# Which products add into their sums by DMA, where x is split, and the order of the last slot, in a three-layer kernel

## The chip, the cores and the metric

The kernel runs on one core of a Trainium2 chip. The metric is the device time of one execution in microseconds, the median of the runs shown. The profile comes from one further execution, taken by the hardware profiler.

## The reference

Linear attention with a normalized output is followed by two layers without biases. The first squares what is left of a ReLU, the second multiplies by a cosine.

```python
kv = np.einsum('bhsd,bhse->bhde', k, v)          # 8 batches, 8 heads, 576 tokens, 64 wide
out = np.einsum('bhsd,bhde->bhse', q, kv)
rms = np.sqrt(np.mean(out * out, axis=-1, keepdims=True) + 1e-06)
x = (out / rms * g_norm)                          # brought to 4608 tokens x 512
h = x @ w_in;  g = np.maximum(h, 0.0) ** 2;  x = g @ w_out      # w_in 512 x 2048
h = x @ w_in2; g = h * np.cos(h);            out = g @ w_out2
```

All of it is float32. The kernel splits operands into a high and a low part and adds up three products (high with high, high with low, low with high).

## The kernel before

**Stage one** runs over nine tiles of 512 tokens and, in each, over parts of the hidden width of the first layer (`layer_in`, `layer_out`, L379 and L416); together they are its chunks. Half of that layer is done here directly, and its partial results are evicted by ScalarE and VectorE into `ev` (L402, L404) and stored to `p_d` (L405). Between the chunks stand the units of attention, whose results `xo` are stored to `x_d`; the conversion of weights, which brings them from their given form into high and low parts and combinations of blocks (L111 to L197); and, for the later token tiles, the loads of x from `x_d` (`load_x`, L227) and the split of x (`split_x`): ScalarE casts the high part (L232), and GpSimd subtracts it from x to give the low part (L233).

**The slots** follow, from about 502 us on: thirty, ten for the rest of the first layer (m=0) and twenty for the second (m=1), each a tile of tokens and one group of the hidden width. The tiles are 512, 512, 512, 384 and 384 wide in one half (there are two halves of each, j). A slot does its matrix products by a scheme with seven products for eight blocks, in the order 0, 1, 3, 2, 5, 4, 6. First products (L508) go into the two banks FA and FB in turn. `keep` (L527), `add` (L533, L537) and `whole` (L545) make four blocks h from them, and ReLU and square (L549, L553) or five steps of the cosine (L557 to L575) make y. They are finished in the order (0,0), (1,1), (0,1), (1,0). `s_block` makes the operand of a second product from the y, with up to two subtractions on VectorE (L591), then splits it: gh is cast by ScalarE (L607), gl subtracted by VectorE (L608). Second products (L631) go into the banks SA and SB in turn, which `drain_product` empties. The operands t1 and t2 of products 2 and 3 are made together, when product 3's operand is due.

`drain_product` has four ways. The first product of many slots is copied by ScalarE into the other bank, as what product 1 then adds to (L650). In the first group of a tile the sums are begun by a copy on ScalarE (L654). Products named in BY_DMA are copied by ScalarE into one of two buffers `part` (L659), and GpSimd issues a DMA that adds them to the sum (L660). All others are added by VectorE (L662). Products 0 and 1 belong to the sum (0,0), 2 and 5 to (1,1), 3 and 4 to (0,1), 6 to (1,0). Only slots with m=1 use the DMA, and the last slot doesn't.

Seven pairs of late weights of the second layer are loaded (L145, SyncE) and converted during the first slots.

**The order.** Every action is given a position on an axis of chunks and slots (`at`, `pos`; PH is a seventh of a slot). Positions are priorities: the order of each engine is set when the program is built, by a scheduler that follows them and its own view of what is ready. SyncE issues nearly all DMAs, in order, so one that waits holds those behind it. Tiles take their memory from pools in the order in which the pools are opened; a tile that takes the memory of another waits until that one has been read.

Of the kernel before, what the change touches and what calls it, by code (L numbers as in the profile page):

```python
# [8 lines left out]
F32 = mybir.dt.float32  # L9
# [4 lines left out]
ALU = mybir.AluOpType  # L14
# [8 lines left out]
def kernel(  # L23
# [205 lines left out]
    def split_x(t, c):  # L229
        h, l = new_x(t, c)  # L230
        src = xraw[t, c // 2][:, c % 2, :]
        nc.scalar.copy(out=h, in_=src)  # L232
        nc.gpsimd.tensor_tensor(out=l, in0=src, in1=as32(h[:]), op=ALU.subtract)  # L233

# [191 lines left out]
    BLOCKS = {(0, 0): 2, (1, 1): 5, (0, 1): 6, (1, 0): 7}  # L426
    S_ORDER = (0, 1, 3, 2, 5, 4, 6)
    BY_DMA = (4, 5, 1, 6)
    SEEDED = 2
# [6 lines left out]

    HOLD = 9
    xb, wi, ws, kept, hs, ys, sums, quads = {}, {}, {}, {}, {}, {}, {}, {}

# [139 lines left out]
    def load_sum(k, d, j):  # L579
# [3 lines left out]
        for b, s0, done, size in pieces(t0 + j * ht, ht, TOK):  # L583
            nc.sync.dma_start(out=e[:, :, done:done + size], in_=p_d[b][:, 2 * d:2 * d + 2, s0:s0 + size])

    def s_block(k, i):
        m, t, q = slots[k]
        b11, b12, b21, b22 = (ys.get((k, b)) for b in ((0, 0), (0, 1), (1, 0), (1, 1)))

        def minus(out, x, y):  # L590
            nc.vector.tensor_tensor(out=out, in0=x, in1=y, op=ALU.subtract)  # L591
            return out

        if i == 3:
            ys[k, "t1"] = minus(t_tile(k, F32, "t"), b12, b11)
            ys[k, "t2"] = minus(t_tile(k, F32, "t"), b22, ys[k, "t1"])
        src = {
            0: lambda: b11,
            1: lambda: b21,
            2: lambda: ys[k, "t1"],  # L600
            3: lambda: ys[k, "t2"],
            4: lambda: b22,
            5: lambda: minus(b12, b22, b12),
            6: lambda: minus(b21, b21, ys[k, "t2"]),
        }[i]()
        gs[k, i] = h, l = [t_tile(k, F32R, f"g{n}") for n in "hl"]
        nc.scalar.copy(out=h, in_=src)  # L607
        nc.vector.tensor_tensor(out=l, in0=src, in1=as32(h), op=ALU.subtract)  # L608
# [77 lines left out]
    class Stream:  # L686
# [10 lines left out]
        def place(self, positions, after, skip=()):  # L697
            for k, (n, item) in enumerate(zip(positions, self.items)):
                steps = (0, 0.07, 0.15, 0.22, 0.3, 0.4, 0.62)
                if n < nA0:  # L700
# [30 lines left out]
    at(pos(0.15), late_stream.advance)  # L731
    late_stream.place([pos(0.45 + 1.05 * k) for k in range(5)] + [pos(9.9), pos(10.85)], 0)

# [15 lines left out]
    for t in range(NDIRECT, NTILE):  # L749
        n0 = t * NH  # L750
        for q in range(2):
            at(n0 - (4 if t == NDIRECT else 5.2) + q, load_x, t, q)
        for c in range(NKC):
# [6 lines left out]
    for k, (m, t, q) in enumerate(slots):  # L760
        if q == 0:
            for a in range(2):
                at(pos(k + (a - 6.8) * PH) if k else nA0 - 9, load_quads, m, t, a)
            for f, i in enumerate(ORDER):
                at(pos(k + X_AT[f] * PH) if k or f > 3 else nA0 - 7 + 1.5 * f, x_block, k, i)
        for f, i in enumerate(ORDER):
            at(pos(k + (f - 2.7) * PH) if k or f > 2 else nA0 - 5 + f / 2, load_wi, k, i)
        for f, i in enumerate(S_ORDER):
            at(pos(k + LAG2 + (f - 2.7) * PH), load_ws, k, i)
            at(pos(k + LAG2 + (f - (1.1 if f == 1 else 1.6)) * PH), s_block, k, i)  # L770
        if not seeded(k):
# [53 lines left out]
    def run_slots():  # L825
# [12 lines left out]
        steps1 = (x for k, i in firsts for x in first_product(k, i))  # L838
        todo = [(k, i) for k in range(len(slots)) for i in S_ORDER]
        steps2 = (x for k, i in todo for x in second_product(k, i))  # L840
# [34 lines left out]
    with ExitStack() as early:  # L875
# [5 lines left out]
        pools["raw"] = right("conv", 2)  # L881
        x_p, g_p, ev_p, pools["t"] = (right(n, b) for n, b in (("x", XB), ("g", 3), ("ev", 2), ("tmp", 8)))
        with tc.tile_pool(name="att", bufs=1, side="right") as att_p:
# [64 lines left out]
```

## Time and profile before

| | us |
|---|---|
| runs, median (lowest, highest) | 1594.09 (1589.73, 1597.51) |
| profiled execution | 1593.9 |
| its span, first to last instruction | 1592.1 |
| TensorE busy | 1542.6 |
| VectorE busy | 1254.8 |
| ScalarE busy | 1107.7 |
| GpSimd busy | 105.5 |

The mean granted clock of TensorE is 0.997 of full speed. To read it: each engine runs its own instructions in order, and semaphores tie them. Idle time of an engine that isn't the bound costs nothing by itself; a wait counts where TensorE has to wait in the end. The rows below give for an instruction its start and length, and in brackets how long its engine stood idle before it and what ended that.

### The profile page before, as it was taken

How to read it: one execution, taken by the hardware profiler on the slowest of the kernel's cores; microseconds unless marked ns; L12 is line 12 of the kernel's file. 1: busy time of each engine (PE TensorE's matmuls, PEld its weight loads, DVE VectorE, ACT ScalarE, POOL GpSimd, SP SyncE). 2: the span in 40 equal slices, each digit the busy share in tenths (PEclk: the TensorE clock that was granted, in tenths of full speed). 3: DMA queues.
4: the chain of work that ended last, by engine and by line, in shares of the span. 5: the costliest groups of instructions: out<-in, count | busy, mean ns of one | idle time of the engine just before them, and what ended most of it. 6: DMA issues, size and time to landing. Idle time of an engine off the chain costs nothing.

```text
span 1592.1 us, 24817 instructions
## 1 busy us (share of the span) xinstructions
PE 1542.6 (97%) x9104; PEld 1349.8 (85%) x9104; DVE 1254.8 (79%) x1676; ACT 1107.7 (70%) x1568; POOL 105.5 (7%) x117
## 2 busy tenths in 40 slices
PE   5999999999999999999999999999999999999997
PEld 4777777778887777888998899999998999999997
DVE  7988788788885898987879868766876687687576
ACT  6977677775444666665656778877887777778774
POOL 1100101111000000000000000000000001011010
PEclk9999999999999999999999999999999999999999
DMA  9758889866678989998999779987998799999994
GB/s 325 269 168 230 261 259 284 238 204 208 195 230 298 309 283 338 319 385 263 336 355 341 279 229 269 280 266 227 268 271 263 227 262 297 333 302 275 323 296 116
DMA packets 229160, 433.13 MB, mean 272 GB/s; under 512 B 18608, under 2 KB 144816, under 8 KB 229040
## 3 DMA queue, kind: packets, MB, share of 16 engines
q1 hardware_dynamic: 218624, 397.21, 74.2%
q0 software_dynamic: 10416, 34.35, 10.7%
q8 instruction: 72, 1.18, 0.3%
q14 instruction: 48, 0.39, 0.1%
HBM read 317.72 MB, written 81.79 MB: 251 GB/s over the span
## 4 chain that ended last, share of the span: by engine, by line
PE 77%; DMA 8%; DVE 6%; issue 4%; ACT 4%; SPq 0%; DVEq 0%; ACTq 0%; POOLq 0%
PE SB L631 14%; PE SA L631 14%; PE FB L508 13%; PE FA L508 13%; PE acc L416 10%; PE l L379 9%; DMA sum<-part 2%; PE o L379 1%; DMA ws_d<-raw 1%; PE ss L379 1%; DVE gl L608 1%; DMA xraw<-x_d 1%; DMA q<-in_qT 1%; DMA p_d<-ev 1%; DMA raw<-in_wA 1%
## 5 line engine op out<-in xcount | busy, mean ns | idle before, releaser
L508 PE MATMUL FA<-xh,wi 128*128 128x512 f32 (+1 forms) x840 | 300.0, 371 | 8.0 <-ACT h L545 3.3
L508 PE MATMUL FB<-xh,wi 128*128 128x512 f32 (+1 forms) x840 | 299.3, 370 | 0.0
L631 PE MATMUL SA<-ws,gh 128*128 128x256 f32 x1008 | 230.3, 282 | 5.5 <-ACT gh L607 5.5
L631 PE MATMUL SB<-ws,gh 128*128 128x256 f32 x1008 | 229.3, 282 | 2.0 <-ACT SB L650 1.9
L631 PEld LDWEIGHTS SA<-ws,gh 128*128 128x128 f32 x1008 | 181.9, 190 | 17.3 <-ACT gh L607 6.2
L631 PEld LDWEIGHTS SB<-ws,gh 128*128 128x128 f32 x1008 | 181.0, 189 | 14.0 <-ACT SB L650 3.3
L508 PEld LDWEIGHTS FA<-xh,wi 128*128 128x128 f32 x840 | 157.3, 188 | 20.5 <-ACT h L545 3.9
L575 DVE SCALAR_TENSOR_TENSOR y<-y,h 128x1024 f32<-128x1024 f32 (+1 forms) x80 | 89.3, 1116 | 108.4 <-ACT y L571 108.1
L508 PEld LDWEIGHTS FB<-xh,wi 128*128 128x128 f32 x840 | 157.3, 188 | 11.1
L631 PE MATMUL SB<-ws,gl 128*128 128x256 f32 x504 | 142.4, 282 | 1.5 <-DVE gl L608 1.5
L631 PE MATMUL SA<-ws,gl 128*128 128x256 f32 x504 | 142.4, 282 | 0.6 <-DVE gl L608 0.6
L608 DVE TENSOR_TENSOR gl<-y,gh 128x1024 fp32r<-128x1024 f32 (+1 forms) x100 | 111.2, 1113 | 34.7 <-ACT gh L607 33.5
L660 POOL DMA_DIRECT2D sum<-part x67 | 57.0, 851 | 1101.9 <-DMA wi<-wi_d 535.2
L557 ACT ACTIVATE y<-h,zerob 128x1024 int32<-128x1024 f32 (+1 forms) x80 | 85.3, 1066 | 40.7 <-DVE h L533 40.6
L416 PE MATMUL acc<-gh,wh 128*128 128x512 f32 x288 | 113.6, 395 | 0.0
L416 PE MATMUL acc<-gl,wh 128*128 128x512 f32 x288 | 112.8, 392 | 0.0
L416 PE MATMUL acc<-gh,wl 128*128 128x512 f32 x288 | 112.6, 391 | 0.0
L508 PE MATMUL FA<-xl,wi 128*128 128x512 f32 (+1 forms) x300 | 111.3, 371 | 0.0
L508 PE MATMUL FB<-xl,wi 128*128 128x512 f32 (+1 forms) x300 | 110.9, 370 | 0.0
L607 ACT CAST gh<-y 128x1024 fp32r<-128x1024 f32 (+1 forms) x100 | 95.0, 962 | 12.6 <-DVE y L575 7.4
L631 PE MATMUL SB<-gh,ws 128*128 128x512 f32 (+1 forms) x280 | 100.0, 370 | 2.9 <-ACT SB L650 1.1
L631 PEld LDWEIGHTS SB<-ws,gl 128*128 128x128 f32 x504 | 95.5, 190 | 7.8 <-DVE gl L608 2.4
(172 smaller groups left out, 3775.4 us busy)
## 6 DMA issues: line engine op xcount, KB each, us to landing
wi<-wi_d SPq DMA_DIRECT2D x210, 512.0 KB, 6.8
ws<-ws_d SPq DMA_DIRECT2D x210, 512.0 KB, 6.0
sum<-part POOLq DMA_DIRECT2D x43, 512.0 KB, 8.1
kvld<-in_kv SPq DMA_DIRECT2D x32, 512.0 KB, 6.7
ws_d<-raw SPq DMA_DIRECT2D x24, 448.0 KB, 4.1
q<-in_qT SPq DMA_DIRECT2D x32, 288.0 KB, 4.0
p_d<-ev SPq DMA_DIRECT2D x18, 512.0 KB, 3.8
sum<-part POOLq DMA_DIRECT2D x24, 384.0 KB, 7.9
```

The source lines that it names most:

```text
L379: nc.tensor.matmul(ps, a[:, 0, cs], m[:], start=(c == 0 and k == 0), stop=(c == NKC - 1 and k == 2))
L416: nc.tensor.matmul(o, a[:, cs], m[:], start=(f == 0 and n == 0), stop=(f == NH - 1 and n == 2), skip_group_check=True)
L508: nc.tensor.matmul(ps[:, pp, :], a, b, start=(n == 0 and (i in (0, 2) or i == 1 and not seeded(k))), stop=(n == 5), skip_group_check=True,)
L557: nc.scalar.activation(out=y.bitcast(I32), in_=hs[k, b], func=AF.Identity, bias=zerob)
L575: nc.vector.scalar_tensor_tensor(out=y, in0=y, scalar=-2.0 * math.pi, in1=hs.pop((k, b)), op0=ALU.add, op1=ALU.mult)
L607: nc.scalar.copy(out=h, in_=src)
L608: nc.vector.tensor_tensor(out=l, in0=src, in1=as32(h), op=ALU.subtract)
L631: nc.tensor.matmul(ps[:, b, :], lhs, rhs, start=(n == 0 and (m == 0 or b % 2 == 0) and (i in (0, 2) or i == 1 and not seeded_s(k))), stop= ...
L660: nc.gpsimd.dma_start(out=e, in_=part, accum_op=ALU.add)
```

## The change

Eight things are changed.

1. `split_x` subtracts the low part on VectorE, 28 instructions.
2. BY_DMA is 1, 2 and 4 in place of 4, 5, 1 and 6. Accumulating DMAs, and the copies to `part` on ScalarE, fall from 67 to 48; VectorE has 19 adds more.
3. The last slot runs its second products in the order 0, 2, 3, 4, 5, 1, 6.
4. t1 and t2 are made by a job of their own, placed ahead of product 2's operand.
5. The late pairs are placed otherwise: the first as before, the others in pairs nearer to each other, and the steps of one conversion closer together.
6. x loads in stage one are placed about a chunk sooner (the first of a tile at 6.2 chunks ahead).
7. The x blocks four to seven of the first slot are placed a seventh of a slot later.
8. The pool of `ev` is opened ahead of those of x, g and the temporaries. With that the late raw buffer shares memory with `ev`.

```diff
-        nc.gpsimd.tensor_tensor(out=l, in0=src, in1=as32(h[:]), op=ALU.subtract)
+        nc.vector.tensor_tensor(out=l, in0=src, in1=as32(h[:]), op=ALU.subtract)
...
-    S_ORDER = (0, 1, 3, 2, 5, 4, 6)
-    BY_DMA = (4, 5, 1, 6)
+    BY_DMA = (1, 2, 4)
...
+    def s_order(k):
+        return ORDER if k < len(slots) - 1 else (0, 2, 3, 4, 5, 1, 6)
...
+    def s_sums(k):
+        ys[k, "t1"] = minus(t_tile(k, F32, "t"), ys[k, (0, 1)], ys[k, (0, 0)])
+        ys[k, "t2"] = minus(t_tile(k, F32, "t"), ys[k, (1, 1)], ys[k, "t1"])
...
-        if i == 3:
-            ys[k, "t1"] = minus(t_tile(k, F32, "t"), b12, b11)
-            ys[k, "t2"] = minus(t_tile(k, F32, "t"), b22, ys[k, "t1"])
...
-                steps = (0, 0.07, 0.15, 0.22, 0.3, 0.4, 0.62)
+                steps = (0, 0.06, 0.12, 0.17, 0.23, 0.3, 0.45)
...
-    late_stream.place([pos(0.45 + 1.05 * k) for k in range(5)] + [pos(9.9), pos(10.85)], 0)
+    late_stream.place([pos(n) for n in (0.4, 2.45, 3.07, 4.45, 5.07, 10.5, 11.1)], 0)
...
-            at(n0 - (4 if t == NDIRECT else 5.2) + q, load_x, t, q)
+            at(n0 - (6.2, 3 if t == 2 else 4.2 if t == 3 else 5.1)[q], load_x, t, q)
...
-                at(pos(k + X_AT[f] * PH) if k or f > 3 else nA0 - 7 + 1.5 * f, x_block, k, i)
+                at(pos(k + (X_AT[f] + (0 if k else 1)) * PH) if k or f > 3 else nA0 - 7 + 1.5 * f, x_block, k, i)
...
-        for f, i in enumerate(S_ORDER):
+        for f, i in enumerate(s_order(k)):
             at(pos(k + LAG2 + (f - 2.7) * PH), load_ws, k, i)
-            at(pos(k + LAG2 + (f - (1.1 if f == 1 else 1.6)) * PH), s_block, k, i)
+            at(pos(k + LAG2 + (f - (1.1 if f == i == 1 else 0.9 if f == 2 and i == 3 else 1.6)) * PH), s_block, k, i)
+            if f == 1:
+                at(pos(k + LAG2 + (0.35 if i == 1 else -0.7) * PH), s_sums, k)
...
-        x_p, g_p, ev_p, pools["t"] = (right(n, b) for n, b in (("x", XB), ("g", 3), ("ev", 2), ("tmp", 8)))
+        ev_p, x_p, g_p, pools["t"] = (right(n, b) for n, b in (("ev", 2), ("x", XB), ("g", 3), ("tmp", 8)))
```

What it does to the order of the engines is shown at three places. In these rows stands the line of the program, which is two or three more in the changed kernel, the operation, output and input, and the semaphores it waits for (DMAHW and DMASW: DMAs issued by SyncE and by GpSimd).

**SyncE at the end of stage one.** `raw<-in_wB` is the load of the next late pair, `p_d<-ev` the stores of the last evictions, `sum<-p_d` and `wi`, `ws` loads for the slots. Before:

```order
L492 DMA ws<-ws_d_0_96 128x1024 [waits DMAHW2_49,PE_49]
L145 DMA raw<-in_wB 128x1024 [waits DMAHW3_49,PE_49,Pool_49]
L145 DMA raw<-in_wB 128x2x512 [waits DMAHW4_49]
L487 DMA wi<-wi_d_1_91 128x1024 [waits DMAHW5_49,PE_49]
L584 DMA sum<-p_d_76 128x1024 [waits DMAHW6_49,PE_49]
L492 DMA ws<-ws_d_0_96 128x1024 [waits DMAHW7_49,PE_49]
L487 DMA wi<-wi_d_1_91 128x1024 [waits DMAHW0_49,PE_49]
L405 DMA p_d_84<-ev 128x1024 [waits DMAHW1_49,DVE_49,Activation_49]
L405 DMA p_d_84<-ev 128x1024 [waits DMAHW2_49,DVE_49,Activation_49]
```

After:

```order
L587 DMA sum<-p_d_76 128x1024 [waits DMAHW4_49,PE_49]
L495 DMA ws<-ws_d_0_96 128x1024 [waits DMAHW5_49,PE_49]
L490 DMA wi<-wi_d_1_91 128x1024 [waits DMAHW6_49,PE_49]
L405 DMA p_d_84<-ev 128x1024 [waits DMAHW7_49,DVE_49,Activation_49]
L405 DMA p_d_84<-ev 128x1024 [waits DMAHW0_49,DVE_49,Activation_49]
L587 DMA sum<-p_d_77 128x1024 [waits DMAHW1_49,PE_49]
L495 DMA ws<-ws_d_0_96 128x1024 [waits DMAHW2_49,PE_49]
L145 DMA raw<-in_wB 128x1024 [waits DMAHW7_49,DMAHW3_49,DMAHW0_49]
L145 DMA raw<-in_wB 128x2x512 [waits DMAHW4_49]
```

The raw load stood ahead of the two stores; now it stands behind them and waits for two more DMAs, those of the two stores (DMAHW7 and DMAHW0).

**ScalarE at the same place.** `ev<-acc` are its evictions, L112, L192 steps of the late conversion, `m` and `u` the kept first products. Before:

```order
L112 ACTIVATE e<-e,expb 128x1024 [waits DVE_49]
L402 COPY ev<-acc_5641 128x512 [waits DMAHW5_49,PE_49]
L402 COPY ev<-acc_5649 128x512 [waits DMAHW6_49,PE_49]
L481 CAST xh<-xraw 128x1024 [waits DMAHW2_49,DMAHW1_49,DMAHW4_49,DVE_49,Activation_49]
L527 ACTIVATE m_5919<-FA 128x1024 [waits PE_49]
L481 CAST xh<-xraw 128x1024 [waits DMAHW7_49,DMAHW0_49]
L549 ACTIVATE h<-h 128x1024 [waits DVE_49]
L553 ACTIVATE h<-h 128x1024 [waits Activation_49]
L527 ACTIVATE u_5959<-FA 128x1024 [waits PE_49]
L481 CAST xh<-xt 128x1024
L192 CAST wh<-raw 128x768 [waits DMAHW4_49,DMAHW3_49]
L527 ACTIVATE m_5995<-FB 128x1024 [waits PE_49]
```

After:

```order
L402 COPY ev<-acc_5641 128x512 [waits DMAHW5_49,PE_49]
L402 COPY ev<-acc_5649 128x512 [waits DMAHW6_49,PE_49]
L530 ACTIVATE m_5914<-FA 128x1024 [waits DVE_49,PE_49,Activation_49]
L484 CAST xh<-xraw 128x1024 [waits DMAHW4_49]
L484 CAST xh<-xraw 128x1024 [waits DMAHW7_49,DMAHW0_49]
L552 ACTIVATE h<-h 128x1024 [waits DVE_49]
L530 ACTIVATE u_5965<-FA 128x1024 [waits PE_49]
L556 ACTIVATE h<-h 128x1024 [waits Activation_49]
L112 ACTIVATE e<-e,expb 128x1024 [waits DMAHW7_49,DMAHW0_49,DVE_49]
L192 CAST wh<-raw 128x768 [waits DMAHW4_49,DMAHW3_49,DVE_49]
L192 CAST wh<-raw 128x1024 [waits DVE_49]
L530 ACTIVATE m_5993<-FB 128x1024 [waits PE_49]
```

The conversion's L112 stood ahead of the evictions and one cast L192 ahead of `m<-FB`; now all three of its steps stand between the second relu step and `m<-FB`, and the first m stands ahead of the two casts of x.

**VectorE in a slot of width 384.** Before, near 1433 us of the profile:

```order
L533 SCALAR_TENSOR_TENSOR h<-FA,u_14334 128x2x384 [waits PE_49]
L608 TENSOR_TENSOR gl<-y,gh 128x2x384 [waits Activation_49]
L482 TENSOR_TENSOR xl<-xt,xh 128x2x384
L561 SCALAR_TENSOR_TENSOR y<-y,h 128x2x384 [waits Activation_49]
L575 SCALAR_TENSOR_TENSOR y<-y,h 128x2x384 [waits Activation_49]
L463 TENSOR_TENSOR xt<-xraw,xt 128x2x384
L575 SCALAR_TENSOR_TENSOR y<-y,h 128x2x384 [waits Activation_49]
L608 TENSOR_TENSOR gl<-y,gh 128x2x384 [waits Activation_49]
```

After, the same place:

```order
L536 SCALAR_TENSOR_TENSOR h<-FA,u_14306 128x2x384 [waits PE_49]
L610 TENSOR_TENSOR gl<-y,gh 128x2x384 [waits Activation_49]
L485 TENSOR_TENSOR xl<-xt,xh 128x2x384
L564 SCALAR_TENSOR_TENSOR y<-y,h 128x2x384 [waits Activation_49]
L578 SCALAR_TENSOR_TENSOR y<-y,h 128x2x384 [waits Activation_49]
L664 TENSOR_TENSOR sum<-SA,sum 128x768 [waits DMASW4_49,PE_49]
L610 TENSOR_TENSOR gl<-y,gh 128x2x384 [waits Activation_49]
L578 SCALAR_TENSOR_TENSOR y<-y,h 128x2x384 [waits Activation_49]
```

Product 5 was copied for the DMA; now its add stands here, behind the cosine step and ahead of gl, and waits for DMASW4, the accumulating DMA of product 2 of the same slot.

## Rows read from the trace of the kernel before

**Rows 1.** The page: busy us, share of the span and count of each engine.

```profile
PE 1542.6 (97%) x9104; PEld 1349.8 (85%) x9104; DVE 1254.8 (79%) x1676; ACT 1107.7 (70%) x1568; POOL 105.5 (7%) x117
```

**Rows 2.** What TensorE waited for: us in total, times, longest us.

```profile
PE SA L631 <- ACT gh L607: 5.5, 3, 3.5
PE ss L316 <- DVE m L329: 4.4, 3, 1.5
PE FA L508 <- ACT h L545: 3.3, 1, 3.3
PE SB L631 <- ACT SB L650: 3.0, 3, 1.5
PE FA L508 <- ACT m L527: 2.8, 2, 1.4
```

**Rows 3.** Timeline, ScalarE: start, us, instruction, [idle before <- what ended it].

```profile
1465.15 0.78 ACT L659 COPY part<-SB 128x768 f32<-128x768 f32 x1
...
1476.50 0.80 ACT L659 COPY part<-SB 128x768 f32<-128x768 f32 x1 [4.88 <-DMA sum<-part]
```

**Rows 4.** Timeline, GpSimd, the same stretch: the issue of an accumulating DMA.

```profile
1466.23 0.85 POOL L660 DMA_DIRECT2D sum<-part  x1 [8.68 <-ACT part L659]
```

**Rows 5.** Stretches: us, busy of five engines, then PEclk, DMA share, GB/s.

```profile
1481.50:1485.50 4.00, 3.96 (x18) 3.96 (x19) 3.90 (x6) 2.45 (x4) 0.00 (x0) 0.61 0.80 205
1571.00:1575.00 4.00, 3.92 (x18) 3.71 (x18) 2.80 (x5) 2.09 (x3) 0.00 (x0) 0.57 0.00 0
```

**Rows 6.** Timeline, SyncE's queue: the last stores of p_d.

```profile
502.70 0.92 SPq L405 DMA_DIRECT2D p_d<-ev  x2
```

**Rows 7.** Timeline, ScalarE: the first cast behind the evictions.

```profile
508.41 1.05 ACT L481 CAST xh<-xraw 128x1024 fp32r<-128x1024 f32 x1 [6.09 <-DMA p_d<-ev]
```

**Rows 8.** Timeline, TensorE: the sixth first product of the first slot begins.

```profile
518.74 0.39 PE L508 MATMUL FB<-xh,wi 128*128 128x512 f32 x1
```

**Rows 9.** Timeline, VectorE: conversion of the first late pair, first and last step.

```profile
499.48 0.69 DVE L111 TENSOR_SCALAR e<-raw 128x1024 uint32<-128x1024 uint32 x1 [3.42 <-PE acc L416]
...
505.66 1.55 DVE L175 TENSOR_TENSOR raw<-raw 128x256 f32<-128x256 f32 x4
```

**Rows 10.** DMA issues: count, KB each, median us from issue to landing.

```profile
sum<-part POOLq DMA_DIRECT2D x43, 512.0 KB, 8.1
...
sum<-part POOLq DMA_DIRECT2D x24, 384.0 KB, 7.9
...
raw<-in_wB SPq DMA_DIRECT2D x14, 512.0 KB, 5.5
```

**Rows 11.** Timeline, TensorE: products 5 and 6 begin, width 512, then 384.

```profile
986.37 0.28 PE L631 MATMUL SA<-ws,gh 128*128 128x256 f32 x1
...
997.57 0.28 PE L631 MATMUL SA<-ws,gh 128*128 128x256 f32 x1
...
1371.32 0.28 PE L631 MATMUL SA<-ws,gh 128*128 128x256 f32 x1
...
1379.76 0.28 PE L631 MATMUL SA<-ws,gh 128*128 128x256 f32 x1
```

**Rows 12.** Timeline, TensorE: waits in the last slot's second products.

```profile
1570.08 0.38 PE L631 MATMUL SA<-ws,gh 128*128 128x256 f32 x1 [3.52 <-ACT gh L607]
1571.07 0.54 PE L631 MATMUL SA<-ws,gl 128*128 128x256 f32 x1 [0.61 <-DVE gl L608]
...
1575.97 0.35 PE L631 MATMUL SA<-ws,gh 128*128 128x256 f32 x1 [0.98 <-ACT gh L607]
```

**Rows 13.** Timeline, VectorE: an add into a sum, width 384.

```profile
1574.91 0.96 DVE L662 TENSOR_TENSOR sum<-SA,sum 128x768 f32<-128x768 f32 x1 [1.17 <-PE SA L631]
```

**Rows 14.** Timeline, VectorE, stage one: conversion steps under a GpSimd subtraction, then gl.

```profile
338.72 1.67 DVE L116 SCALAR_TENSOR_TENSOR w<-raw,w 128x512 uint32<-128x512 uint32 x1
340.31 1.78 DVE L122 SCALAR_TENSOR_TENSOR e<-raw,e 128x512 uint32<-128x512 uint32 x1
342.02 0.68 DVE L394 TENSOR_TENSOR gl<-g,gh 128x512 fp32r<-128x512 f32 x1
```

More of the change, by code (lines that the diff above doesn't have):

```diff
@@ L584, in load_sum, with minus @@
             nc.sync.dma_start(out=e[:, :, done:done + size], in_=p_d[b][:, 2 * d:2 * d + 2, s0:s0 + size])
+    def minus(out, x, y):
+        nc.vector.tensor_tensor(out=out, in0=x, in1=y, op=ALU.subtract)
+        return out
+    def s_sums(k):
+        ys[k, "t1"] = minus(t_tile(k, F32, "t"), ys[k, (0, 1)], ys[k, (0, 0)])
+        ys[k, "t2"] = minus(t_tile(k, F32, "t"), ys[k, (1, 1)], ys[k, "t1"])
     def s_block(k, i):
-        m, t, q = slots[k]
         b11, b12, b21, b22 = (ys.get((k, b)) for b in ((0, 0), (0, 1), (1, 0), (1, 1)))
-        def minus(out, x, y):
-            nc.vector.tensor_tensor(out=out, in0=x, in1=y, op=ALU.subtract)
-            return out
-        if i == 3:
-            ys[k, "t1"] = minus(t_tile(k, F32, "t"), b12, b11)
-            ys[k, "t2"] = minus(t_tile(k, F32, "t"), b22, ys[k, "t1"])
         src = {
@@ L838, in run_slots @@
         steps1 = (x for k, i in firsts for x in first_product(k, i))
-        todo = [(k, i) for k in range(len(slots)) for i in S_ORDER]
+        todo = [(k, i) for k in range(len(slots)) for i in s_order(k)]
         steps2 = (x for k, i in todo for x in second_product(k, i))
```

## The prediction

> **What bounds the kernel now.** I read the shares of busy time first, then what TensorE waits for, and from there the stretches around each wait. TensorE is busy 97% of the span, VectorE 79%, ScalarE 70%, GpSimd 7% [rows 1]. The number of matmuls doesn't change, so the time can only move by what TensorE waits and by the clock it gets. Its waits that the change can touch come to 19 us, in five kinds [rows 2]: 5.5 us for the cast gh, 4.4 us for m of the attention units, 3.3 us for one h, 3.0 us for the copy of SA into SB, 2.8 us for m of the first products. Those 19 us and the clock lost behind them, some 1.4%, are all that can be won, and every new wait on TensorE counts against them in full.
>
> The longest of them behind stage one has its cause three steps away. ScalarE's copy of a second product into `part` at 1476.50 waited 4.88 us for an accumulating DMA [rows 3]; that DMA was issued at 1466.23 [rows 4], so it took 10.3 us to land. Everything that stands behind the copy on ScalarE is late, h among it, and TensorE waits 3.3 us for that [rows 2]. Then the granted clock is 0.61 over four microseconds [rows 5], which is the lower of its two levels for most of them and costs 4 x 0.39 = 1.6 us more. The same shows at the end, where a wait of 3.52 us is followed by a clock of 0.57 [rows 5, 12], 1.7 us.
>
> **Stage one: subtractions and x loads.** 28 subtractions go to VectorE at about 0.68 us, the time of gl, a subtraction of the same shape [rows 14]: 19 us of its time are added. Some comes back. L116 at 338.72, under a GpSimd subtraction, took 1.67 us, gl a little later 0.68 [rows 14]. If each of the 28 lengthened one such instruction by 1.0 us, moving them would give VectorE 28 us for 19; if none did, it would cost 19. On TensorE's path lie only the three waits for m, 4.4 us in all. Just behind these rows stands one of them, and there two lengthened instructions (1.0 and 1.1 us) shrink, two subtractions (1.4 us) come, and the order puts m ahead of one conversion step (0.7 us): that wait of about 1.3 us goes. The other two hang on an x load that TensorE's units don't see sooner: SyncE's order moves x loads past one pair of x_d stores in five places only, and the cast xh that waits now stands ahead of the subtraction on VectorE. Term: **-1.3 us**, bounds -4.4 (all three go) and +2 (VectorE then waits for late casts with m behind it).
>
> The Trainium skill, SBUF — State Buffer, section Who interferes with whom, says that a VectorE instruction with two SBUF inputs contends with a GpSimd instruction that reads SBUF. The 1.67 us beside 0.68 us agree with it [rows 14]. By that rule the term is -1.3 us; without it, with nothing given back, the two subtractions would outweigh the earlier m and it would be about +0.7 us.
>
> **Into the slots.** A load moves from ahead of the last evictions to behind them. Before, the raw load of the next late pair had landed by 499.48, when L111 uses it [rows 9]. Now it stands on SyncE behind both p_d<-ev stores and waits for them to land, because its buffer shares their memory. They were issued at 502.70 [rows 6] and had landed at 508.41, when the xh waiting for them ran [rows 7]. The evictions no longer share their engines with the conversion, so I take 1 us off: 507.4. A raw load of this size takes 5.5 us [rows 10]: 512.9. VectorE's steps L111 to L175 took 499.48 to 507.21, less 1.28 us for the two evictions among them, 6.4 us [rows 9]: 519.3. On ScalarE the casts of that conversion now stand ahead of m<-FB: three instructions of nearly 1 us, as the xh of 1.05 us there [rows 7]: 522. That m frees the bank FB, whose next product started at 518.74 [rows 8]. Without this wait it would now start some 2.4 us sooner, since 1 us at the evictions and one of the two waits for m (1.4 us [rows 2]), behind the xh that waited 6.09 us [rows 7], are gone. So TensorE idles from 516.3 to 522, 5.7 us, and as behind the waits of 3.3 and 3.5 us I charge 1.6 us of clock. Against before: 522 + 1.6 - 518.74 = **+4.9 us**. Bounds: -2.4 if the load is no longer a matter, +7.5 if it takes 8.1 us, as the accumulating ones do. What is queued behind it: on SyncE x and wi loads, which the banks hold up anyway; on VectorE xl of the next x blocks.
>
> The second late load has the same shape a slot later with more slack: VectorE's L111 now stands ahead of gl and waits some 4 us. Against that the second wait for m (1.4 us) and small ones near it lose their cause. Term **0**, bounds -3 and +4.
>
> **Sums.** BY_DMA falls from four products to three, 67 accumulating DMAs to 48. They are products 1, 2 and 4, every second of the order, and never three in a row; a `part` buffer is then used again no sooner than four products on, twice the 8.4 us that two take [rows 11], against 10.3 us of that DMA. The wait of 4.88 us goes with its h and its clock: 3.3 + 1.6 = **-4.9 us**. ScalarE loses 19 copies; VectorE gets 19 adds of about 1 us over 700 us, which it has room for. The copies of SA into SB stood behind casts of t on ScalarE; t1 and t2 are now made earlier in the slot. Of 3.0 us I take **-2.5**, bounds -3 and 0. Of the waits for gh 5.5 - 3.52 - 0.98 = 1.0 us stands in the first slot of m=1 beside the last conversion, which moves later: **-1.0**, bounds -1 and +1.
>
> But there is a new tie. Products 2 and 5 add into the same sum and follow each other. 2 now goes by DMA and 5 by VectorE, so the add of 5 must wait until the DMA of 2 has landed; and as long as it waits, the bank is not free for product 6. In a slot of width 384: copy to issue 1.1 us [rows 3, 4], 7.9 us to landing [rows 10], add 0.96 us [rows 13], with 0.1 us to start 10.0 us behind the end of 2. TensorE starts 5 there, at 1371.32, and wants the bank at 1379.76, 8.4 us later [rows 11]. It waits 1.6 us. Four slots outside the tail have this: **+6.4 us**. Bounds: 0 with a landing in 6.3 us, 16 with the 10.3 us of the slowest. In a slot of width 512, copy and add a third longer: 0.1 + 1.3 + 8.1 [rows 10] + 1.2 = 10.7 us, against 986.37 to 997.57, 11.2 us [rows 11]: **0** now, but with 0.5 us to spare in nine slots; 10.3 us would cost 1.7 us each, 15 us.
>
> **Tail.** The last slot now takes the product of the last block that is finished (1) sixth, not second. Before, TensorE waited 3.52, 0.61 and 0.98 us there, at the lower clock between [rows 12, 5]. Product 2 needs t1, thus the block before, but the add of slot 28's product 5 now waits for its DMA too and holds VectorE about 2 us, with t1 behind it. So product 2 starts about where product 1 did, at 1570.4 for 1570.08; what goes is what came after: 0.61 + 0.98 + 1.7 of clock. Term -3.3 + 0.3 = **-3.0**, bounds -6.8 (the first wait too) and +2.
>
> **Sum.** -1.3 + 4.9 + 0 - 4.9 - 2.5 - 1.0 + 6.4 - 3.0 = -1.4 us. The profiled execution took 1593.9 us, the median of the runs 1594.09: **1592.5 us**, no change that a measurement of this kernel can tell, which takes about 0.5%, 8 us.
>
> **Rivals.**
> 1. Faster: one of the two new waits isn't there. If the accumulations land within 6.3 us, for which fewer of them and no two close together speak, 6.4 us are saved: 1586. If the raw load is hidden, 7.3 us: 1585. Both: 1579. Against it stand the medians of 7.9 and 5.5 us.
> 2. Slower: the tie of 5 to 2. From a landing of 9 us on it decides: 5 x 1.1 in the narrow slots (the tail's with them) and 9 x 0.4 in the wide ones give +9, 1601.6; at 9.5 us it is 1592.5 + 5 x 1.6 + 9 x 0.9 = 1608.6. For it: one of 10.3 us is in the trace, and a copy that starts late on ScalarE acts like a late landing. Against it: that one ran beside two neighbours, which are gone.
> 3. The x loads and the order in the slots don't do what they say: stage one gives nothing, and the second and third late loads repeat the first at half its price (2.5 us each): 1592.5 + 1.3 + 5 = 1599.
>
> **How the numbers follow.** The forecast, 1587 to 1598: 0.47. Faster (1), 1578 to 1586: 0.25. Slower (2), 1602 to 1612: 0.18. The third, within 0.5%: 0.10. So faster 0.25, the same 0.57, slower 0.18. Cutting half a tenth below and a tenth above, the range is 1580 to 1606.
>
> **What would show it.** Right: a TensorE wait of 5 to 6 us for m<-FB near 516, and L111 waiting for raw just ahead; no ScalarE wait for an accumulating DMA; VectorE sums in the 384 slots waiting for sum<-part, and behind each a TensorE wait of 1 to 2 us on the bank; at the end one wait and then products without a gap. Wrong: sums that never wait (then 1), sums waiting in the 512 slots with TensorE behind them (then 2), or no wait near 516.

## The result, and the profile after

| | before | after |
|---|---|---|
| runs, median (lowest, highest), us | 1594.3 (1589.73, 1597.51) | 1607.74 (1600.82, 1611.05) |
| profiled execution, us | 1593.9 | 1604.13 |
| its span, us | 1592.1 | 1602.3 |
| mean granted clock | 0.997 | 0.990 |

The ratio is 1.0081 (95% interval 1.0059 to 1.0103): the changed kernel is slower by 0.8%, where the forecast was 1592.5 us and no change, and it lies 1.7 us above the range. It is the sign of rival 2. The medians are of eight runs of each kernel. Of the 13.4 us between them the profiled executions show 10.2; the traces are read against those.

The page of the changed kernel, busy us of each engine, answers [rows 1]: GpSimd has half its work left, VectorE has 21 us more, ScalarE 14 us less.

```profile
PE 1547.3 (97%) x9104; PEld 1354.7 (85%) x9104; DVE 1275.6 (80%) x1723; ACT 1093.9 (68%) x1549; POOL 51.7 (3%) x70
```

What TensorE waited for, changed kernel (us in total, times, longest), answers [rows 2]. The largest row, a DMA at the start of the kernel, is about the same in both and left out. The waits for h and for the copy of SA into SB, 3.3 and 3.0 us before, no longer stand among the largest; 8.5 us for m<-FB and 3.6 us for a copy into FA are new.

```profile
...
PE FB L511 <- ACT m L530: 8.5, 1, 8.5
PE FA L511 <- ACT FA L543: 3.6, 4, 1.0
...
PE SB L633 <- issue: 2.6, 1, 2.6
...
PE SB L633 <- ACT gh L609: 2.1, 1, 2.1
PE SA L633 <- ACT y L574: 2.0, 1, 2.0
```

Behind the copy stands a row on VectorE, from 870 us to the end of the changed kernel, that the kernel before does not have at all:

```profile
DVE sum L664 <- DMA sum<-part: 33.8, 12, 5.5
```

**Where the time went.** The number and order of first products are the same in both kernels, so the start of the same product in both traces shows where the 10.2 us arose. "Predicted" sums the terms that belong to the stretch. Each column is one execution: up to slot 10 the kernel with BY_DMA = (1, 4) of the experiments runs the same instructions as the changed one, and its slots 1 to 9 took 314.0 us where the changed kernel took 311.9. Differences of 2 us in a stretch can be chance.

| up to the start of | before | after | difference | in this stretch | predicted |
|---|---|---|---|---|---|
| slot 0 | 503.34 | 502.12 | -1.2 | -1.2 | -1.3 |
| slot 1 | 524.18 | 531.79 | +7.6 | +8.8 | |
| slot 10 | 839.33 | 843.72 | +4.4 | -3.2, so +5.6 from slot 0 on | +4.9 |
| slot 12 | 914.77 | 922.73 | +8.0 | +3.6 | -1.0 |
| slot 24 | 1376.66 | 1391.89 | +15.2 | +7.3 | 0 |
| slot 29's second first product | 1536.26 | 1550.22 | +14.0 | -1.3 | +6.4 - 4.9 |
| the end of the span | 1592.1 | 1602.3 | +10.2 | -3.8 | -3.0 |

(The term of -2.5 for the copies of SA into SB is spread over the slots.) The second products that run from the start of slot 12 to the start of slot 24 are nearly all 512 wide (called the 512-wide slots below), and there the prediction had nothing.

**What happens in the 512-wide slots.** The chain of work that ended last, changed kernel, in one such slot (start, us, what):

```profile
956.87 7.14 DMA sum<-part
964.11 0.93 DVE sum L664
965.25 0.83 DVE y L578
966.09 0.30 issue
966.38 1.22 DVE gl L610
967.60 1.14 DVE y L564
968.77 1.06 ACT y L570
969.83 0.92 ACT FA L543
970.79 0.50 PE FA L511
```

The accumulating DMA of product 2 lands after 7.1 us. The add of product 5 on VectorE waits for it, and the instructions behind it in VectorE's order wait with it: the cosine steps L578 and L564, which have nothing to do with the sum. ScalarE's L570 waits for L564; behind L570 stands ScalarE's copy of the first product from FB into FA, and TensorE's next first product waits for that copy. The same place in the timeline of the changed kernel (start, us, instruction, [idle before <- what ended it]):

```profile
964.11 1.22 DVE L664 TENSOR_TENSOR sum<-SB,sum 128x1024 f32<-128x1024 f32 x1 [3.03 <-DMA sum<-part]
...
968.77 1.06 ACT L570 ACTIVATE y<-y 128x1024 f32<-128x1024 f32 x1 [1.39 <-DVE y L564]
969.73 1.01 ACT L543 COPY FA<-FB 128x1024 f32<-128x1024 f32 x1
...
970.79 0.50 PE L511 MATMUL FA<-xh,wi 128*128 128x512 f32 x1 [0.80 <-ACT FA L543]
```

VectorE was ready for the add at 964.11 - 3.03 = 961.08, so the DMA had 4.2 us from its issue where it takes 7. Seven of the nine 512-wide slots with this pair wait so, 2.1 to 5.5 us each; VectorE reaches the add 4.2 to 5.1 us after the issue, and the landings take 6.5 to 9.8 us. In the other two VectorE reaches it about 7.0 us after the issue (996.89 and 1156.83), and TensorE doesn't wait there, though the copy stands behind L570 all the same. One of them:

```profile
996.89 0.85 POOL L662 DMA_DIRECT2D sum<-part  x1 [8.44 <-ACT part L661]
...
1003.98 1.23 DVE L664 TENSOR_TENSOR sum<-SA,sum 128x1024 f32<-128x1024 f32 x1
...
1009.11 1.07 ACT L570 ACTIVATE y<-y 128x1024 f32<-128x1024 f32 x1
1010.07 1.02 ACT L543 COPY FB<-FA 128x1024 f32<-128x1024 f32 x1
```

The worst wait is where the widths change. There the landing took 9.8 us, and the bank itself is late too:

```profile
1351.93 0.85 POOL L662 DMA_DIRECT2D sum<-part  x1 [7.50 <-ACT part L661]
...
1361.78 1.22 DVE L664 TENSOR_TENSOR sum<-SB,sum 128x1024 f32<-128x1024 f32 x1 [5.47 <-DMA sum<-part]
...
1363.10 0.36 PE L633 MATMUL SB<-ws,gh 128*128 128x256 f32 x1 [2.59 <-issue]
...
1365.64 0.84 ACT L570 ACTIVATE y<-y 128x768 f32<-128x768 f32 x1 [4.08 <-DVE y L564]
```

The profile calls the releaser of 1363.10 "issue", but the add that frees SB ends at 1361.78 + 1.22 = 1363.0. Five 384-wide adds wait 1.0 to 3.1 us.

**Into the slots**, timeline of the changed kernel:

```profile
501.03 1.37 SPq L405 DMA_DIRECT2D p_d<-ev  x2
...
507.52 1.62 SPq L145 DMA_DIRECT2D raw<-in_wB  x2
...
515.87 0.69 DVE L111 TENSOR_SCALAR e<-raw 128x1024 uint32<-128x1024 uint32 x1 [5.17 <-DMA wi<-wi_d]
...
523.40 1.02 ACT L530 ACTIVATE m<-FB 128x1024 f32<-128x1024 f32 x1
...
524.47 0.79 PE L511 MATMUL FB<-xh,wi 128*128 128x512 f32 x1 [8.46 <-ACT m L530]
```

The raw load is issued at 507.52, where 507.4 was predicted, since it waits for the stores. L111 starts 8.35 us later, 5.5 were predicted; m<-FB ends at 524.4, 522 were predicted. (The releaser shown for L111 is another DMA; L111 reads only raw.) The pair comes in two loads (x2), the second issued 0.4 us behind the first, and here it took 7.8 us from its own issue. So TensorE waits 8.5 us, not 5.7. In five other kernels with the same order here (BY_DMA = (1, 5, 6), (1, 4), and three more of the experiments) the second load took 5.8 to 6.2 us and TensorE waited 6.7 to 7.2 us.

**Slot 11**, timeline of the changed kernel, the last late conversion and the operand of a second product:

```profile
892.30 1.56 DVE L175 TENSOR_TENSOR raw<-raw 128x256 f32<-128x256 f32 x4
894.34 0.96 DVE L194 TENSOR_TENSOR raw<-raw,wh 128x768 fp32r<-128x768 f32 x1 [0.49 <-ACT wh L192]
895.28 1.23 DVE L610 TENSOR_TENSOR gl<-y,gh 128x1024 fp32r<-128x1024 f32 x1
...
893.47 0.83 ACT L192 CAST wh<-raw 128x768 fp32r<-128x768 f32 x1
894.21 1.05 ACT L609 CAST gh<-y 128x1024 fp32r<-128x1024 f32 x1
...
895.30 0.39 PE L633 MATMUL SB<-ws,gh 128*128 128x256 f32 x1 [2.09 <-ACT gh L609]
896.56 0.39 PE L633 MATMUL SB<-ws,gl 128*128 128x256 f32 x1 [0.88 <-DVE gl L610]
```

Its steps stand right ahead of gh on ScalarE and of gl on VectorE, and TensorE waits for both.

**Tail**, timeline of the changed kernel, answers [rows 12]: one wait, and from there no gap in TensorE's work.

```profile
1575.18 0.96 DVE L664 TENSOR_TENSOR sum<-SA,sum 128x768 f32<-128x768 f32 x1 [1.02 <-DMA sum<-part]
...
1581.72 0.95 DVE L664 TENSOR_TENSOR sum<-SA,sum 128x768 f32<-128x768 f32 x1
...
1582.77 0.42 PE L633 MATMUL SA<-ws,gh 128*128 128x256 f32 x1 [1.98 <-ACT y L574]
```

The profile names L574 on ScalarE, but what ends the wait is the bank: the add of slot 28's product 6, which VectorE makes in the changed kernel, frees SA at 1581.72 + 0.95 = 1582.67.

### The profile page after: what moved, and what is told of

It is laid out like the page before. It is cut to its first block, busy times and chain, and to the rows that moved or that the text cites. A ratio compares the mean times of both kernels' runs of the same rounds, so it can differ in the third digit from the quotient of the medians.

```text
span 1602.3 us, 24673 instructions
## 1 busy us (share of the span) xinstructions
PE 1547.3 (97%) x9104; PEld 1354.7 (85%) x9104; DVE 1275.6 (80%) x1723; ACT 1093.9 (68%) x1549; POOL 51.7 (3%) x70
## 4 chain that ended last, share of the span: by engine, by line
PE 44%; issue 34%; DVE 9%; DMA 8%; ACT 3%; POOL 1%; SPq 1%; POOLq 0%; DVEq 0%; ACTq 0%
PE acc L416 11%; PE l L379 9%; PE SA L633 5%; PE FA L511 5%; PE FB L511 5%; PE SB L633 5%; DMA sum<-part 2%; DVE gl L610 1%; DMA wi<-wi_d 1%; DMA q<-in_qT 1%; DVE sum L664 1%; PE o L379 1%; POOL sum L662 1%; DMA ws<-ws_d 1%; DMA ws_d<-raw 1%
## 5 line engine op out<-in xcount | busy, mean ns | idle before, releaser
L610 DVE TENSOR_TENSOR gl<-y,gh 128x1024 fp32r<-128x1024 f32 (+1 forms) x100 | 111.2, 1113 | 38.8 <-ACT gh L609 38.7
L578 DVE SCALAR_TENSOR_TENSOR y<-y,h 128x1024 f32<-128x1024 f32 (+1 forms) x80 | 89.0, 1113 | 35.2 <-ACT y L574 35.0
L570 ACT ACTIVATE y<-y 128x1024 f32<-128x1024 f32 (+1 forms) x80 | 77.9, 973 | 54.2 <-DVE y L564 54.1
L664 DVE TENSOR_TENSOR sum<-SB,sum 128x1024 f32<-128x1024 f32 (+1 forms) x62 | 69.0, 1113 | 55.2 <-DMA sum<-part 29.5
```

Source lines behind the costliest of these rows:

```text
L570: nc.scalar.activation(out=y, in_=y, func=AF.Sin, scale=math.pi)
L578: nc.vector.scalar_tensor_tensor(out=y, in0=y, scalar=-2.0 * math.pi, in1=hs.pop((k, b)), op0=ALU.add, op1=ALU.mult)
L664: nc.vector.tensor_tensor(out=e, in0=ps, in1=e, op=ALU.add)
```

## The experiments

The theory after the result: the tie of product 5's add to product 2's DMA costs most, through VectorE's order. Its rivals: the 19 more adds on VectorE cost by themselves; the raw load and the late conversions are the main part; the subtraction of low parts. All times are medians; the kernel before stood at 1595.2 to 1596.3 us beside these runs. Kernels that are compared weren't all measured together; by their ratios to the kernel before, the differences given here move by up to 2.4 us, most by less than 1.

**Without the tie.** Products 5 and 6 go by DMA, as they did before, and 2 and 4 by VectorE; there are as many DMAs and adds as in the changed kernel. Each of 1, 5 and 6 is the last of its slot in its sum; 2 isn't, since 5 follows in the same sum.

```diff
-    BY_DMA = (1, 2, 4)
+    BY_DMA = (1, 5, 6)
```

> The changed kernel with BY_DMA = (1, 5, 6) in place of (1, 2, 4): as many accumulating DMAs, copies and adds (48), but no product whose add by VectorE follows the DMA of its neighbour into the same sum. Theory 1 (the tie of product 5's add to product 2's DMA is the main loss): VectorE's waits for sum<-part (33.8 us in 12 places from 870 us on) go, the TensorE waits of about 1 us at the second first product of the slots of m=1 (FA copy, 8 places) and the 2.6 us near 1363 go with them; 8 to 11 us less than the changed kernel, about 1597. Theory 2 (the adds cost by their number, 19 more on VectorE): no change, 1607. Theory 3 (the late raw load is the main loss): no change, and the wait of 8.5 us near 524 stays.

Measured: 1590.13 us, ratio to before 0.9963 (0.9951 to 0.9974), 17.6 us less than the changed kernel, more than the 8 to 11 expected. No add waits for an accumulating DMA. At the place shown above the copy into FA now stands ahead of L570 on ScalarE, and TensorE doesn't wait; timeline of this kernel:

```profile
970.28 1.00 ACT L543 COPY FA<-FB 128x1024 f32<-128x1024 f32 x1 [1.06 <-PE FB L511]
971.93 1.06 ACT L570 ACTIVATE y<-y 128x1024 f32<-128x1024 f32 x1 [0.65 <-DVE y L564]
```

Against this kernel the changed one is 2.6 us ahead at the start of slot 12, which is chance, since up to slot 10 both run the same instructions; it is 7.4 behind at the start of slot 24, and 12.5 behind at the end. So in its profiled execution 10.0 us are lost in the 512-wide slots, 4.4 of them in the slot where the widths change, and 5.1 behind them (3.2 in the 384-wide slots, 1.8 in the tail).

**More adds on VectorE.** Against the changed kernel only product 2 goes another way. If the 14 adds that leave DMA cost, this is slower than the last.

```diff
-    BY_DMA = (1, 2, 4)
+    BY_DMA = (1, 4)
```

> The changed kernel with BY_DMA = (1, 4): product 2 is added by VectorE as 5 is, so the tie is gone, and VectorE has 14 to 16 adds more than in the changed kernel, ScalarE as many copies fewer. Theory 1 (the tie costs, adds by their number don't): within 3 us of e1, 1588 to 1593, and no VectorE wait for sum<-part. Theory 2 (adds cost by their number): above the changed kernel, 1610 and more.

Measured: 1589.44 us, 0.9951 (0.9932 to 0.997). That is 18.3 us less than the changed kernel. VectorE has 14 adds more and is busy 1289.9 us, and the time isn't longer: not the number of adds but the tie. The last slot's wait is still 2.00 us at 1567.80, so the 1.98 us of the changed kernel there are not the tie's; in both VectorE adds product 6.

**The tie alone, in the kernel before.** Two kernels that are the kernel before but for BY_DMA.

```diff
-    BY_DMA = (4, 5, 1, 6)
+    BY_DMA = (1, 2, 4)
```

> The kernel before with BY_DMA = (1, 2, 4) alone. Theory 1 (the tie): VectorE waits for sum<-part in the slots of m=1, with TensorE waits of about 1 us in many of them; against the kernel before it loses 5 to 10 us by them and wins about 5 at 1481 (the wait of ScalarE's copy for a part buffer): 1594 to 1600. If the tie costs nothing, only the win is left: 1589.

Measured: 1602.72 us, 1.0042 (1.0026 to 1.0059), 2.7 us above the upper end expected.

```diff
-    BY_DMA = (4, 5, 1, 6)
+    BY_DMA = (1, 5, 6)
```

> The kernel before with BY_DMA = (1, 5, 6) alone, to stand beside e4 (the same kernel with 1, 2 and 4: 1602.7): same number of DMAs, no tie. The tie is then worth the difference. Expected 1588 to 1590: the wait of 4.9 us of ScalarE's copy near 1476 goes, and with it 3.3 us of TensorE and 1.6 us of clock. If three DMAs close together (5, 6 and the next 1) still fill the two part buffers: a wait for sum<-part on ScalarE stays and the time is within 2 us of before.

Measured: 1591.33 us, 0.9967 (0.9951 to 0.9983). Between the two lie 11.4 us, the price of the tie without the rest of the change. Of the 11.0 us between their profiled executions 3.9 arise in the 512-wide slots, 5.3 in the 384-wide ones and 2.7 in the tail (the first was 0.8 us ahead at slot 12). In the first the same row appears among VectorE's waits,

```profile
DVE sum L662 <- DMA sum<-part: 33.3, 12, 3.9
```

and the same chain in its timeline:

```profile
959.66 1.23 DVE L662 TENSOR_TENSOR sum<-SB,sum 128x1024 f32<-128x1024 f32 x1 [3.41 <-DMA sum<-part]
...
964.32 1.06 ACT L567 ACTIVATE y<-y 128x1024 f32<-128x1024 f32 x1 [1.76 <-DVE y L561]
965.28 1.00 ACT L540 COPY FA<-FB 128x1024 f32<-128x1024 f32 x1
...
966.34 0.50 PE L508 MATMUL FA<-xh,wi 128*128 128x512 f32 x1 [1.18 <-ACT FA L540]
```

The second is 5.0 us under the kernel before: the wait of 4.88 us at 1476.50 [rows 3] is gone with the fourth DMA product.

**The raw load.** The pool of `ev` is opened where it was, in the changed kernel and in the one without the tie.

```diff
-        ev_p, x_p, g_p, pools["t"] = (right(n, b) for n, b in (("ev", 2), ("x", XB), ("g", 3), ("tmp", 8)))
+        x_p, g_p, ev_p, pools["t"] = (right(n, b) for n, b in (("x", XB), ("g", 3), ("ev", 2), ("tmp", 8)))
```

> The changed kernel with the pool of ev opened behind those of x and g again, as before the change; the raw load of the late pair then stands ahead of the evictions' stores on SyncE once more. Theory 3 (the raw load behind the stores): TensorE's wait of 8.5 us near 524 goes, and of the 4.0 us that the changed kernel is behind at the third slot about 4 to 7 come back: 1600 to 1603. Theory 1 (the tie): the later losses stay as they are, and if the raw load's wait were given back by what comes after it, the total stays at 1607.

Measured: 1602.31 us, 1.005 (1.003 to 1.007), 5.4 us under the changed kernel with intervals that overlap. The wait near 524 us is gone, but of 10.3 us won at the start of slot 1, 1.5 of which stood at slot 0 already, only 6.1 are left at slot 10.

> e1 (BY_DMA = (1, 5, 6)) with the pool of ev opened last again: the raw load alone, without the tie beside it. The wait of 7 us near 524 goes. If what follows gives none of it back: 1580 to 1583. If, as in e2, a third to a half of it comes back as waits near 600 to 700: 1584 to 1586.

Measured: 1585.48 us, 0.993 (0.9913 to 0.9948), 4.65 us under the same kernel with the raw load tied. TensorE's largest wait left in slot 0 is then

```profile
510.54 0.50 PE L511 MATMUL FA<-xh,wi 128*128 128x512 f32 x1 [1.08 <-ACT m L530]
```

**Late conversions.** First the last two places alone, in the changed kernel:

```diff
-    late_stream.place([pos(n) for n in (0.4, 2.45, 3.07, 4.45, 5.07, 10.5, 11.1)], 0)
+    late_stream.place([pos(n) for n in (0.4, 2.45, 3.07, 4.45, 5.07, 9.9, 10.85)], 0)
```

> The changed kernel with the last two late conversions at their places before the change (9.9 and 10.85 slots for 10.5 and 11.1). The loss at the twelfth slot (2.1, 0.9 and 1.1 us of waits near 895 to 906 and the lower clock behind them) is put down to the last conversion, which now stands ahead of gh and gl of the first m=1 slot: if so, 3 to 5 us less, 1603 to 1605, and no wait over 1 us there. If the loss comes from something else (the copy sum<-SA ahead of gh on ScalarE), the waits stay and the time too.

Measured: 1604.64 us, 1.0057 (1.0036 to 1.0078). In the trace slot 11 gives back 2.7 us; a wait of 1.46 us at 895.30 stays, where none over 1 us was expected. The medians differ by 3.1 us with intervals that overlap. Then this, the old pool order and (1, 5, 6) together:

> The changed kernel with BY_DMA = (1, 5, 6), the pool of ev opened last as before the change, and the last two late conversions at 9.9 and 10.85 slots. If the three losses stand in different places and add up: e1 (1590) less 5 (e2) less 3 (e3), about 1582, and faster than the kernel before by over 10 us. If one hides another (the raw load's gain is partly given back by stalls near 600): 1585 to 1588.

Measured: 1583.19 us, 0.9915 (0.9898 to 0.9932). The largest wait left in its slots is on the second late conversion, near 604 us: L112 on ScalarE, one of its steps, stands ahead of a cast that TensorE needs.

```profile
603.70 0.76 PE L633 MATMUL SA<-gh,ws 128*128 128x512 f32 x1 [2.78 <-ACT e L112]
```

So all places and the steps of a conversion were put back, in that kernel:

```diff
-                steps = (0, 0.06, 0.12, 0.17, 0.23, 0.3, 0.45)
+                steps = (0, 0.07, 0.15, 0.22, 0.3, 0.4, 0.62)
...
-    late_stream.place([pos(n) for n in (0.4, 2.45, 3.07, 4.45, 5.07, 9.9, 10.85)], 0)
+    late_stream.place([pos(0.45 + 1.05 * k) for k in range(5)] + [pos(9.9), pos(10.85)], 0)
```

> e5 with all late conversions and their steps placed as before the change. What is left of the change is then the split on VectorE, the x loads, the earlier t1 and t2, the last slot's order and BY_DMA (1, 5, 6). If the new places cost (waits of 2.8 us near 604 and 0.9 near 620 in e5): 1580 to 1582. If they win elsewhere: 1584 to 1587, with the waits of before at 550, 560 and 569 back.

Measured: 1575.86 us, 0.9872 (0.9849 to 0.9894), 7.3 us under the last, which is more than expected, and the fastest of all: 1.3% under the kernel before. By the starts of the slots the new places and steps win 3.2 us in slot 1 and lose 6.1 in slot 3, some 2.4 in slots 4 and 5 and 3.0 in slot 11, where only the steps differ. Part of it is the clock: in the kernel of 1583.19 us the granted clock is 0.57 over 603.4 to 607.4 us and over 893.5 to 897.5, and here it is 1.00 in both stretches.

**x loads.** The old places, in the fastest kernel:

```diff
-            at(n0 - (6.2, 3 if t == 2 else 4.2 if t == 3 else 5.1)[q], load_x, t, q)
+            at(n0 - (4 if t == NDIRECT else 5.2) + q, load_x, t, q)
```

> e11 (1575.9) with the x loads of stage one at their places before the change. The prediction held that the new places bring TensorE's units nothing. If so: within 2 us of e11, 1574 to 1578, and the waits near 194 and 199 as they are. If the sooner loads win something: the waits for xh on ScalarE near 191 grow, and the time is 1578 to 1580.

Measured: 1577.69 us, 0.9894 (0.9873 to 0.9914). The intervals overlap: 1.8 us, which this doesn't tell from nothing.

**Low parts of x on GpSimd**, in the kernel with (1, 5, 6):

```diff
-        nc.vector.tensor_tensor(out=l, in0=src, in1=as32(h[:]), op=ALU.subtract)
+        nc.gpsimd.tensor_tensor(out=l, in0=src, in1=as32(h[:]), op=ALU.subtract)
```

> e1 (BY_DMA = (1, 5, 6)) with the low parts of x in stage one subtracted on GpSimd again. The prediction put the move of the subtractions at -1.3 us: with it undone 1591 to 1592, with conversion steps of 1.5 us and more on VectorE under the GpSimd subtractions again and one wait of 1.4 us for m more. If the move costs (VectorE stands behind late casts of x): below 1590, with fewer waits near 197 and 250.

Measured: 1590.22 us, 0.9965 (0.9952 to 0.9979), beside 1590.13 with them on VectorE: nothing.

**Order of the last slot**, in the kernel with (1, 5, 6):

```diff
-        return ORDER if k < len(slots) - 1 else (0, 2, 3, 4, 5, 1, 6)
+        return ORDER
```

> e1 (BY_DMA = (1, 5, 6)) with the second products of the last slot in the old order 0, 1, 3, 2, 5, 4, 6. The tail of e1 won about 4 us against before in its profile; the prediction had 3.3 us of waits and clock behind the first wait, and 3.5 for that. If the order does it: 1593 to 1596 with a wait of some 3 us for gh of product 1 in the last slot. If the earlier t1 and t2 and the lighter ScalarE do it: within 1 us of e1, 1590.

Measured: 1595.66 us, 0.9995 (0.9984 to 1.0007): the new order is worth 5.5 us. With the old one TensorE's waits of [rows 12] come back; timeline of this kernel:

```profile
1571.08 0.38 PE L633 MATMUL SA<-ws,gh 128*128 128x256 f32 x1 [2.78 <-ACT gh L609]
1572.07 0.39 PE L633 MATMUL SA<-ws,gl 128*128 128x256 f32 x1 [0.61 <-DVE gl L610]
...
1576.02 0.55 PE L633 MATMUL SA<-ws,gh 128*128 128x256 f32 x1 [0.64 <-ACT gh L609]
```

## Why the prediction was wrong

**The step that failed is the tie in the 512-wide slots, taken at 0.** The pair, its cause and its direction were seen, and rival 2 was made of it. But the prediction asked only when TensorE wants the bank again, 11.2 us behind the start of product 5, and found 0.5 us to spare. That much is so: in the slot shown the add ends at 965.3 and nothing waits for SB. What it didn't ask is when VectorE reaches the add, and what stands behind it there. In the slot shown VectorE reaches it 4.2 us after the issue of the DMA, which lands after 7.1. The order of VectorE that was read for a 384-wide slot has L610 and L578 behind the add; from there one had to go on to L564, L570 and the copy into FA on ScalarE. In the 512-wide slots the tie cost 10.0 us in the changed kernel's trace and 3.9 in that of the kernel before with (1, 2, 4), for the 0 of the sum. In all the runs price it at 17.6 us in the changed kernel and at 11.4 us in the one before, where the prediction had +6.4.

**Rival 2's condition held in one slot only, although its sign came.** It was to decide from a landing of 9 us on, and its 1608.6 us, for 9.5 us, are close to the 1607.74 measured; but landings became shorter on the whole. DMA issues of the changed kernel (count, KB each, median us to landing), to be read beside [rows 10] with 8.1 and 7.9 us:

```profile
sum<-part POOLq DMA_DIRECT2D x31, 512.0 KB, 7.2
...
sum<-part POOLq DMA_DIRECT2D x17, 384.0 KB, 6.7
```

In the slot where the widths change the landing did take 9.8 us; there the late bank (2.59 us) and the clock behind it (1.7) make up most of the 4.4 us. In the other six waiting 512-wide slots the landings took 6.5 to 7.4 us, and what was lost came through VectorE's order. So rival 2's number came near by luck, for the most part on another path, and the chance of 0.18 was too small: a wait that holds an engine in order needed no long landing.

**In the 384-wide slots, +6.4,** the mechanism was right. The bank wait of 1.6 us each came as 0.5 to 0.8 us in all four slots of this trace (1425.38, 1455.69, 1486.75, 1547.35), behind landings of 6.1 to 6.9 us and not 7.9. The profile gives other releasers, but each time the add of product 5 ends 0.1 us ahead. In the trace of the changed kernel with the old pool order the four waits are 1.0 to 2.5 us, 6.0 in all, and in those of the late conversions' last two places put back and of the kernel before with (1, 2, 4) 4.5 and 4.6 in all: the size was near.

**Late conversions, taken at 0 and, in slot 11, at -1.0.** This is the second term of the wrong size. The bound of +4 was too near: the new places and steps cost 7.3 us in the kernel with (1, 5, 6) and the old pool order, and slot 11 alone +3.6 in the changed kernel's trace. The prediction read one conversion closely and took the others as slack; "moves later" was counted as a gain without asking what it moves next to.

**Into the slots, +4.9.** Right in place, cause and sign. The wait was 8.5 us in the profiled execution and 6.7 to 7.2 in five others with the same order, where 5.7 was predicted: the sum had one load of 5.5 us, and the pair comes in two, of which the second counts. At slot 1 the trace shows +8.8 - 1.2 = +7.6, the upper bound. Of that 3.5 us came back in slot 1, whose waits for m and behind it lost their cause, as the prediction expected of them. The net, by the run without the tied load, is 4.65 us.

**The buffer wait at 1476, -4.9.** Right: -4.5 us at the place in the traces, 5.0 us between the kernel before and the same with three DMA products. No copy on ScalarE waits for an accumulating DMA any more, where before it was 13.0 us in eight places.

**Tail, -3.0.** Right in form, one wait and then no gap; 5.5 us by the run with the old order. The first wait became 1.98 us, not some 3.5, and it is for the bank, not for gh.

**Stage one, -1.3.** The trace gives -1.2, but two executions can't tell that: with the same stage one, slot 0 began anywhere from 500.6 to 503.7 us in nine traces with the change, and from 503.3 to 506.9 in three without it. Moving the subtractions is worth nothing by its own run (0.1 us). The row from which the gain was argued [rows 14] is an extreme: the 50 instructions L116 of this shape took 729 ns on average before and 687 after. Over all of VectorE's instructions in the first 500 us that the two kernels differing in this alone have in common, GpSimd's subtractions cost 14 us, half of the 28 supposed, against 19.3 us for the subtractions on VectorE. The Trainium skill, SBUF — State Buffer, section Who interferes with whom, says that a VectorE instruction with two SBUF inputs contends with a GpSimd instruction that reads SBUF. The traces agree in sign, by 41 ns of L116's mean (729 and 688) in these two kernels, and the prediction's fault was to take one pair of rows for all.

**Copies of SA into SB, -2.5.** The waits left for them are 0.34 and 0.33 us (1497.35, 1557.94). But in the kernel before with BY_DMA = (1, 5, 6), which has the old t1 and t2, 1.1 of the 3.0 us is left: most of it goes with BY_DMA alone. No run changed the job of t1 and t2 alone, so its worth isn't shown.

**What stays open.** Between the changed kernel and the one without the tie lie 17.6 us of medians and 12.5 of the two profiled executions. The rest is where these executions lie: 3.6 us (1604.13) under their median in the changed kernel and 1.5 us (1591.65) above it in the other. Why the order puts the copy into FA behind L570 where the tie is, and ahead of it where it isn't, wasn't tried apart from the tie; the two slots without a wait show only that the order costs TensorE nothing when the add doesn't wait. Why single landings take 9.8 us (the one issued at 1351.93) beside a median of 7.2 isn't known. The fastest kernel lies 20.4 us under the one before; the fourth DMA product (5.0) and the tail (5.5) are shown, and the rest isn't told apart: no run sets back the job of t1 and t2 or the x blocks of the first slot (change 7).

## What to carry to other kernels

An engine that waits for an accumulating DMA holds everything behind it in its order, so the room for the landing is counted up to when that engine reaches the next access to the same sum, not up to when its bank is wanted; give the DMA those products that are the last of their slot in their sum, here 5 or 6 rather than 2. Read what stands behind a new wait on its engine for at least three instructions, and then who waits for those. Opening pools in another order can tie a load to a store that has nothing to do with it, and a load that comes in parts must be priced at the landing of its last part, here 6 to 8 us, not at the median of one, 5.5.

## What the runs showed of the hardware

TensorE's clock fell to its lower level after shorter waits than the 3.3 and 3.5 us of the kernel before. Stretches of the changed kernel behind waits of 2.09, 2.59 and 1.98 us (us, busy of five engines, then the granted clock):

```profile
896.80:900.80 4.00, 4.00 (x19) 3.66 (x19) 4.00 (x4) 2.32 (x3) 0.00 (x0) 0.57 0.87 314
1364.40:1368.40 4.00, 4.00 (x23) 4.00 (x22) 1.62 (x3) 2.31 (x3) 0.00 (x0) 0.57 1.04 277
1582.90:1586.90 4.00, 4.00 (x22) 4.00 (x23) 3.43 (x5) 0.37 (x1) 0.00 (x0) 0.57 0.00 0
```

That is 4 x 0.43 = 1.7 us more for each, as much as behind the longer waits of before. The length of one wait doesn't settle it: the first of these was followed by one of 0.88 us, and behind a wait of 1.46 us at 895.30 in the kernel with the last two places put back the clock stayed at 1.00. The prediction charged the clock only where it expected waits of over 3 us. Accumulating DMAs of 512 KB landed in 5.6 to 10.7 us in the changed kernel; their medians are 7.2 to 7.8 us in the kernels with 48 or fewer of them, against 8.1 us with 67.
